# Last Q tile of chunk 0 placed around the shift products, chunk 3's side lists rebuilt, row tile 2's sums ahead of the norms, 17 fillers for 19

## The chip, the cores and the metric

The kernel runs on one core of a Trainium2 chip. The metric is the device time of one execution in microseconds. TensorE (PE) multiplies, its weight loads (PEld) run beside it; VectorE (DVE), ScalarE (ACT) and GpSimd (POOL) work on vectors; the queue of SyncE (SP) issues nearly all transfers, in order. The engines run beside each other, each takes its own instructions strictly in the order of the program, and they wait for each other by semaphores.

## The reference

One block of an adaptive-layernorm transformer, bf16: S = 2048 rows, D = 1024, F = 3584, 32 heads of 32.

```python
mod = (_silu(c) @ w_mod).reshape(c.shape[0], 6, 1, -1)
sa, ca, ga, sb, cb, gb = ...
h = _layernorm(x) * (1 + ca) + sa
q, k, v = h @ wqkv, split into heads
phi = lambda t: where(t > 0, t + 1, exp(t)) + 1e-06
o = (phi(q) @ (phi(k).T @ v)) / (phi(q) @ phi(k).sum(rows) + 1e-06)
x = x + ga * (o @ wo)
h = _layernorm(x) * (1 + cb) + sb
x = x + gb * ((silu(h @ w_gate) * (h @ w_up)) @ w_down)
```

The change touches the first layernorm and the Q and K projections with `phi`.

## The kernel before

**Tiles and stages.** The 2048 rows are 16 row tiles of 128 and 4 chunks of 512 columns of the transposed activations. `XRES` holds the rows; each row tile is normalized in place and transposed into `HT`, which has two buffers: chunk 0 and 2 in one, 1 and 3 in the other. `dt` counts the 8 slices of D. The scale and shift of the layernorm (`MODCOL`) are applied to the transposed tiles.

**The order.** The program is written out by hand, one instruction after another; a helper (`auto`, whose line L176 every row of the profile bears) records it, and `resolve` turns overlaps of SBUF ranges and uses of a PSUM bank into semaphore waits. A PSUM bank that another engine last used is waited for, whoever wrote or read. What stands first in the program stands first in the queue of its engine.

**Start (lines 628 to 661).** Fillers (`warm`, a 128x512 matmul of zeros) keep TensorE at work while the first four row tiles land. Tiles 0 and 2 get their sums on VectorE (`bn_stats` twice, an aggregate), tiles 1 and 3 on ScalarE (`act_stats`, two passes). `ln1_rstd1` and `ve_sums` send the variance to GpSimd for the power; `ln1_xn` and `ln1_xn_sum` are the norms; `tile_transposes` brings a tile to PSUM on TensorE. `mod_sc` computes columns of the modulation vector with one-column matmuls into bank 0, and `fin_ca`, `fin_sa` copy them out.

**Chunk 0, Q (`q_phase_chunk0`, line 773).** Seven Q tiles accumulate side by side in seven banks (`qb`) while scale and shift become known slice by slice; `q_part` is one Q tile times some slices. The slices 0 to 3 are multiplied unshifted; their shift enters as a bias from `bias_mm` (one-column matmuls into bank 0) and `bias_fin`. The eighth Q tile follows in bank 0. `h0_shift` shifts the slices for K. `q_phi` evacuates a Q tile on ScalarE (Exp, Relu), `q_min` and `q_add` finish it on VectorE. Row tiles 4 to 7 are normalized here and transposed by the DMA (`th_dma`).

**Chunk 0's K, then chunks 1 to 3.** A group is eight 512-column matmuls, 1.73 us. Chunk 0 has 8 K groups, each other chunk 8 K and 8 Q groups. `phi_evac` puts Exp (and Relu for Q) on ScalarE into one of four slots of `E1`; after every second group `phi_flush` finishes both on VectorE, for K with an instruction that reads PSUM and writes `PKT`. `next_bank` (line 703) says which PSUM bank a group gets.

**Side lists.** After group `gi`, the functions of the lists `kside`, `s1`, `s2`, `s3` under that number are written into the program (line 870): statistics and norms of later row tiles (`ln_half`, `ln1_xn`), their transposes, `th_mod` (scale and shift of a transposed slice, for chunk 3 on VectorE for even slices and ScalarE for odd ones), `macc` (a matrix-vector product for a further piece of the modulation vector, on VectorE), `macc_split` (its split into two bf16 parts and their transpose), loads of weights.

Of the kernel before, what the change touches and what calls it, by code (L numbers as in the profile page):

```python
# [5 lines left out]
FP32 = mybir.dt.float32  # L6
# [256 lines left out]
def bass_adaLN_cond__linear_attn_block__swiglu_ffn__prompt_kernel(  # L263
# [22 lines left out]
    with ExitStack() as es:  # L286
# [6 lines left out]
        def T(name, off, shape, dt):  # L293
            n = 1
            for s_ in shape[1:]:
                n *= s_
            assert off % 32 == 0 and off + n * mybir.dt.size(dt) <= ARENA, (name, off, shape)
            return nc.alloc_sbuf_tensor_at(name, shape, dt, offset=base + off)
# [47 lines left out]
        RL = T("rl", 188 * KB, [128, 4, 512], BF16)  # L346
        E1X = T("e1x", 192 * KB, [128, 4, 512], BF16)
        RLX = T("rlx", 196 * KB, [128, 4, 512], BF16)
        ACC = T("acc", 192 * KB, [128, D], FP32)
        MHL = T("mhl", 196 * KB, [128, 2, D], BF16)  # L350
        MHLT = T("mhlt", 192 * KB, [128, 2 * NDT, 128], BF16)
# [105 lines left out]
        def warm(n=1, bank=2):  # L457
            for _ in range(n):
                P.pe("matmul", out=PS[:, bank, :], lhsT=IDENT[:], rhs=E1[:, 0, :], start=True, stop=True)
# [23 lines left out]
        def ln1_xn(st, c0=0, c1=D):  # L483
            P.dve("tensor_scalar", out=XRES[:, st, c0:c1], in0=XRES[:, st, c0:c1],
                  scalar1=MV[:, st, 0:1], scalar2=RSTD[:, st:st + 1], op0=ALU.subtract, op1=ALU.mult)
# [22 lines left out]
        def mod_sc(w, c0, ms, kts=range(NDT)):  # L508
            for m in ms:
                for kt in kts:  # L510
                    P.pe("matmul", out=PS[:, 0, c0 + m:c0 + m + 1], lhsT=w[:, kt, m * 128:(m + 1) * 128],
                         rhs=SILUC[:, kt:kt + 1], start=mod_first[0], stop=(kt == NDT - 1), skip_group_check=True)
                    mod_first[0] = False
# [48 lines left out]
        def ln1_rstd1(st):  # L562
            P.dve("tensor_scalar", out=VE[:, st:st + 1], in0=MV[:, st, 1:2], scalar1=EPS, scalar2=None, op0=ALU.add)
            P.pool("tensor_tensor", out=RSTD[:, st:st + 1], in0=VE[:, st:st + 1], in1=NEGHALF[:, 0:1], op=ALU.pow)
# [58 lines left out]
        def ve_sums(st):  # L623
            P.dve("tensor_scalar", out=VE[:, st:st + 1], in0=SUMSQ[:, st:st + 1], scalar1=MV[:, st, 1:2], scalar2=EPS,
                  op0=ALU.add, op1=ALU.add)
            pool_pow(st)

        warm(13, bank=3)
        act_stats(1)
        act_stats(3)  # L630
        for f in s0_:
# [1 line left out]
        ln1_rstd1(0)  # L633
        msq_neg(1)
        s2_[0]()
        ln1_xn(0)
        tile_transposes(0)
        warm(5, bank=3)
        ve_sums(1)
        s2_[1]()  # L640
        s2_[2]()
        ln1_rstd1(2)
        ln1_xn_sum(1)
        tile_transposes(1)
        warm(1, bank=3)
        msq_neg(3)
        ln1_xn(2, 0, 512)
        ve_sums(3)
        ln1_xn(2, 512, D)
        tile_transposes(2)  # L650
        mod_sc(WCA, 8, range(2))
        ln1_xn_sum(3, 0, 512)
        ln1_xn_sum(3, 512, D)
        fin_ca(0, 2)
        tile_transposes(3)
        mod_sc(WCA, 8, range(2, 4))
        h0_first(0, "dve")
        h0_first(1, "dve")
        raw_copy(4, "dve")
# [43 lines left out]
        def next_bank():  # L703
            i = qk_ctr[0]
            qk_ctr[0] += 1
            return (1, 2, 3, 4, 6, 7, 5, 0)[i % 8] if i < 40 else i % 5 + 1

        def q_group(ch, nt):
            buf, bank = ch % 2, next_bank()
# [39 lines left out]
        def mod_row_b(bank, i, dst):  # L749
# [3 lines left out]
            P.wait_for("sp", [wr])  # L753
            P.dma("mdr%d" % i, dst[:], MDR[i].unsqueeze(0).to_broadcast([128, D]))

        def q_slot(nt):
            return (E1, RL) if nt < 4 else (E1X, RLX)

        def q_phi(nt, bank):
            for buf, fn_ in zip(q_slot(nt), (ACT.Exp, ACT.Relu)):  # L760
                P.act("activation", out=buf[:, nt % 4, :], in_=PS[:, bank, :], func=fn_, bias=BIASQ[:, nt:nt + 1])

        def q_min(nts):
            for nt in nts:
                e = q_slot(nt)[0][:, nt % 4, :]
                P.dve("tensor_scalar", out=e, in0=e, scalar1=1.0, scalar2=1e-6, op0=ALU.min, op1=ALU.add)

        def q_add(nts):
            for nt in nts:
                e, r = q_slot(nt)  # L770
                P.dve("tensor_tensor", out=PQT[:, nt, 0:512], in0=r[:, nt % 4, :], in1=e[:, nt % 4, :], op=ALU.add)

        def q_phase_chunk0():
            qb = [1, 2, 3, 4, 6, 7, 5]
            fin_ca(2, 2)
            for dt in (2, 3):
                h0_first(dt, "dve")
            for nts, dts in ((range(3), (0,)), (range(3), (1,)), ((3, 4, 5, 6), (0, 1))):
                for nt in nts:
                    q_part(nt, qb[nt], dts)  # L780
            for nt in range(7):
                if nt == 4:
                    mod_sc(WCA, 8, range(4, 8))
                    fin_ca(4, 4)
                    for dt in (4, 5):
                        h0_scale_only(dt)
                q_part(nt, qb[nt], (2, 3))
            act_stats(4, (0,))
            for nt in range(7):
                if nt == 6:  # L790
                    mod_sc(WSA, 0, range(6, 8))
                    fin_sa(6, 2)
                    for dt in (6, 7):
                        h0_scale(dt)
                q_part(nt, qb[nt], (4, 5))
            mod_sc(WSA, 0, range(4, 6))
            fin_sa(4, 2, True)
            for dt in (4, 5):
                h0_shift(dt)
            for nt in range(7):  # L800
                if nt == 2:
                    bias_mm((4, 5))
                q_part(nt, qb[nt], (6,))
            for nt in range(7):
                if nt == 1:
                    mod_sc(WSA, 0, range(4), range(4))
                if nt == 3:
                    mod_sc(WSA, 0, range(4), range(4, 8))
                    fin_sa(0, 4, True)
                    ln_ops[1][0]()  # L810
                if nt == 5:
                    bias_mm(range(4))
                    bias_fin()
                q_part(nt, qb[nt], (7,))
            ln_ops[1][1]()
            ln_ops[1][2]()
            ln1_rstd1(5)
            for i, dt in enumerate((4, 5, 0, 1, 2, 3, 6, 7)):
                P.pe("matmul", out=PS[:, 0, :], lhsT=WQK[:, dt, 896:1024], rhs=HT[:, 0, dt, :], start=(i == 0),
                     stop=(i == 7))  # L820
            for dt in range(4):
                h0_shift(dt)
            ln1_xn(5)
            th_dma(5)
            for nt in range(2):
                q_phi(nt, qb[nt])
            act_stats(4, (1,))
            for nt in range(2, 8):
                q_phi(nt, qb[nt] if nt < 7 else 0)
            for f in ln_ops[2]:  # L830
                f()
            act_var(4)
            pool_pow(4)
            for f in ln_ops[3]:
                f()
            ln1_rstd2(6)
            ln1_xn_sum(4)
            th_dma(4)
            q_min((0, 1))
            for st in (6, 7):  # L840
                ln1_xn(st)
                th_dma(st)
            q_add((0, 1))
            for nts in ((2, 3), (4, 5)):
                q_min(nts)
                q_add(nts)
            qk_ctr[0] = 0

        def add(d, k, f):
# [2 lines left out]
        kside = {}  # L852
        ln_ops = [ln1_stats_ops(4 + jj) for jj in range(4)]

        for c0 in (0, 256):
            for dt in range(NDT):
                add(kside, 1, lambda dt=dt, c0=c0: th_mod(1, dt, c0, c0 + 256))
        add(kside, 1, lambda: q_min((6, 7)))
        add(kside, 1, lambda: q_add((6, 7)))
        for jj, k in ((0, 3), (1, 4)):  # L860
            add(kside, k, lambda jj=jj: act_stats(10 + jj))
        q_phase_chunk0()
        for st in range(12, 16):
# [44 lines left out]
            add(s1, 2, lambda jj=jj: th_dma(8 + jj))  # L908
        for i, dt in zip([9, 9, 10, 10, 10, 11, 11, 11], range(NDT)):
            add(s1, i, lambda dt=dt: th_mod(2, dt))  # L910
        ln_half(3, s1, 8, 8, 11)
        for jj in range(4):
            add(s1, 13 + jj // 2, lambda jj=jj: ln1_xn(12 + jj))
            add(s2, 0, lambda jj=jj: th_dma(12 + jj))
        for dt in range(NDT):
            add(s2, 6 + dt, lambda dt=dt: th_mod(3, dt))
        for kt in range(NDT):
            add(s2, 4 + kt, lambda kt=kt: macc(STG, kt))
        add(s2, 13, macc_split)
        add(s2, 13, lambda: P.dma("stg1", STG[:], wmv[:, :, 4096:5120]))  # L920
        for kt in range(NDT):
            add(s3, 4 + kt, lambda kt=kt: macc(STG, kt))
        add(s3, 14, macc_split)
        add(s1, 7, lambda: P.pool("memset", ap=MROW[:], constant=0.0))
        add(s1, 7, lambda: P.pool("memset", ap=ZHL[:], constant=0.0))
        s3.setdefault(2, []).extend([mod_red, mod_row_a])
        add(s3, 12, lambda: mod_row_b(7, 0, GA_B))
        add(s3, 10, z_cols)
        chunk(1, s1)
# [326 lines left out]
```

## Time and profile before

| what | us |
|---|---|
| median of 3 runs | 827.82 (827.47 to 1765.51) |
| the profiled execution, its own time | 828.25 |
| its span, first to last instruction | 826.5 |
| TensorE busy | 821.8 |
| VectorE busy | 313.4 |
| ScalarE busy | 197.0 |
| GpSimd busy | 41.0 |

The span is cut into the start (to 12.2 us), chunk 0's Q (to 29.9), chunk 0's K (to 43.7), chunks 1, 2 and 3 (to 71.5, 99.1 and 126.8), the rest of the attention (to 195) and the gated feed-forward. A row of a timeline names its start, its length, the engine, the operation, what it writes and reads, and how many instructions are merged. Busy times are unions of spans; a matmul's span is longer than the spacing of two matmuls, since they are pipelined.

### The profile page before, as it was taken

Reading aid. Unit: us, or ns where it says so; the run is one execution under the profiler, and the core shown is the slowest. Engines: PE = TensorE matmul, PEld = TensorE weight load, DVE = VectorE, ACT = ScalarE, POOL = GpSimd, SP = SyncE. Lnnn points to the kernel's source line nnn. Section 1 sums busy time; section 2 is a strip of 40 time slices with the busy share of each in tenths; the row PEclk is TensorE's granted clock in tenths of the full one; section 3 lists DMA queues with packets and bytes.
Section 4 is the critical chain, followed back from the end, with each engine's and each line's share of the span. In section 5 each row is a group of like instructions: output and inputs, shape, how many; then the busy total and the mean of one; then the engine's idle time right before and its main releaser. Section 6 shows DMA issues by size and latency. Waiting matters only on the chain.

```text
span 826.5 us, 10519 instructions
## 1 busy us (share of the span) xinstructions
PE 821.8 (99%) x4322; PEld 376.3 (46%) x4322; DVE 313.4 (38%) x672; ACT 197.0 (24%) x338; POOL 41.0 (5%) x58
## 2 busy tenths in 40 slices
PE   8999999999999999999999999999999999999998
PEld 4544444444444444444444444444444444444444
DVE  5798988566945521121221112122111211221111
ACT  4658643223341111011111101111110111111011
POOL 1110000000130000020000003000000300000000
PEclk9999999999999999999999999999999999999999
DMA  9969666865697985600455580045557004553000
GB/s 314 289 144 222 167 165 147 178 177 205 155 255 241 296 249 152 169 26 26 134 152 151 151 177 25 20 133 152 151 153 182 27 19 125 152 152 87 0 26 26
DMA packets 199456, 119.32 MB, mean 144 GB/s; under 512 B 58088, under 2 KB 183152, under 8 KB 199408
## 3 DMA queue, kind: packets, MB, share of 16 engines
q1 hardware_dynamic: 199392, 118.65, 53.7%
q8 instruction: 34, 0.56, 0.3%
q14 instruction: 14, 0.11, 0.0%
q10 hardware_dynamic: 16, 0.00, 0.0%
HBM read 100.67 MB, written 4.33 MB: 127 GB/s over the span
## 4 chain that ended last, share of the span: by engine, by line
PE 98%; DMA 1%; ACT 0%; SPq 0%; DVE 0%; POOL 0%; issue 0%
PE ps L176 98%; DMA xres<-in_A_x_dram 1%; ACT ht L176 0%; SPq L176 0%; DVE xres L176 0%; POOL rstd L176 0%; DVE ve L176 0%
## 5 line engine op out<-in xcount | busy, mean ns | idle before, releaser
L176 PE MATMUL ps<-h2t,guu 128*128 128x512 bf16 x896 | 211.7, 379 | 0.0
L176 PE MATMUL ps<-h2t,gug 128*128 128x512 bf16 x896 | 211.7, 379 | 0.0
L176 DVE TENSOR_TENSOR at<-sg,ps 128x512 bf16<-128x512 bf16 x112 | 77.1, 688 | 282.7 <-PE ps L176 281.1
L176 ACT ACTIVATE sg<-ps 128x512 bf16<-128x512 f32 x112 | 66.9, 597 | 309.7 <-PE ps L176 309.7
L176 PEld LDWEIGHTS ps<-h2t,guu 128*128 128x128 bf16 x896 | 87.7, 98 | 105.7
L176 PEld LDWEIGHTS ps<-h2t,gug 128*128 128x128 bf16 x896 | 87.6, 98 | 105.5
L176 PE MATMUL ps<-wd_a,at 128*128 128x512 bf16 (+1 forms) x512 | 112.4, 377 | 0.0
L176 PE MATMUL ps<-ht,wqk 128*128 128x512 bf16 x512 | 112.1, 379 | 0.0
L176 PE MATMUL ps<-wd_b,at 128*128 128x512 bf16 (+1 forms) x384 | 85.0, 377 | 0.0
L176 DVE TENSOR_TENSOR ut<-att,gb_b 128x512 bf16<-128x512 bf16 (+1 forms) x32 | 14.6, 456 | 166.5 <-ACT att L176 166.5
L176 PEld LDWEIGHTS ps<-wd_a,at 128*128 128x128 bf16 x512 | 50.1, 98 | 59.7
L176 PEld LDWEIGHTS ps<-ht,wqk 128*128 128x128 bf16 x512 | 49.2, 98 | 58.9 <-DVE ht L176 1.0
L176 ACT ACTIVATE att<-ps 128x512 bf16<-128x512 f32 (+1 forms) x32 | 17.4, 591 | 182.1 <-PE ps L176 182.1
L176 PEld LDWEIGHTS ps<-wd_b,at 128*128 128x128 bf16 x384 | 37.6, 98 | 44.7
L176 PE MATMUL ps<-pk,xres 128*128 128x512 bf16 x256 | 56.2, 379 | 0.0
L176 PE MATMUL ps<-mw,pqt 128*128 128x512 bf16 x256 | 55.9, 379 | 0.0
L176 POOL TENSOR_SCALAR h2t<-h2t,modcol 128x512 bf16<-128x512 bf16 x32 | 26.4, 841 | 382.9 <-DMA h2t<-xn 382.9
L176 ACT ACTIVATE e<-ps 128x512 bf16<-128x512 f32 x56 | 33.3, 611 | 31.8 <-PE ps L176 16.3
L176 ACT ACTIVATE junk<-xres 128x1024 bf16<-128x1024 bf16 x26 | 27.6, 1063 | 46.5 <-DVE xres L176 34.2
L176 PEld LDWEIGHTS ps<-mw,pqt 128*128 128x128 bf16 x256 | 24.8, 98 | 30.0 <-issue 0.5
L176 PEld LDWEIGHTS ps<-pk,xres 128*128 128x128 bf16 x256 | 24.7, 98 | 29.9 <-issue 0.9
L176 DVE SCALAR_TENSOR_TENSOR xres<-ps,xres 128x512 bf16<-128x512 f32 x32 | 21.5, 688 | 11.5 <-PE ps L176 11.3
(111 smaller groups left out, 339.3 us busy)
## 6 DMA issues: line engine op xcount, KB each, us to landing
gug<-in_B_w_gate_dram SPq DMA_DIRECT2D x56, 512.0 KB, 3.9
guu<-in_B_w_up_dram SPq DMA_DIRECT2D x56, 512.0 KB, 5.2
xres<-in_A_x_dram SPq DMA_DIRECT2D x20, 256.0 KB, 4.3
stgx<-in_w_mod_dram SPq DMA_DIRECT2D x2, 2048.0 KB, 9.9
wd_a<-in_B_w_down_dram SPq DMA_DIRECT2D x4, 1024.0 KB, 7.2
out_dram<-xres SPq DMA_DIRECT2D x31, 128.0 KB, 1.7
rb<-recip_den SPq DMA_DIRECT2D x8, 384.0 KB, 8.7
xres<-in_A_x_dram SPq DMA_DIRECT2D x3, 1024.0 KB, 6.8
```

The costliest lines, as they stand in the source:

```text
L176: return getattr(e, method)(**kw)
```

## The change

- Start: 14 fillers ahead instead of 13, then 1 and 2 instead of 5 and 1. VectorE does the second half of tile 2's sums, tile 1's variance and tile 2's variance ahead of the norm of tile 0. Three instead of two columns of the scale are computed ahead of tile 3's transposes.
- Q tile 7 of chunk 0: it no longer has bank 0 but Q tile 0's, which ScalarE copies out to a new fp32 buffer `QRAW`; the shift products and the bias products are placed among its eight matmuls instead of among the seven last parts. Both ScalarE passes of row tile 4 come behind that copy, and its variance ahead of the bias. The Q tiles are evacuated in the order 1 to 7, 0.
- Behind them only two pairs of Q tiles are finished ahead of K; the other two come after K group 3. `th_mod(1)` has 12 instructions instead of 16. ScalarE's sums of tiles 10 and 11 come one K group later.
- `next_bank` has another order for the first 40 groups.
- The statistics of tiles 12 to 15 move from groups 8 to 11 of chunk 1 to groups 12 to 14, their norms to group 15 and chunk 2's group 0, their transposes behind group 1, `th_mod(3)` from chunk 2's groups 6 to 13 to groups 4 to 11. The split of the first `macc` moves from group 13 to 12, with the load that follows ahead of it; in chunk 3 `mod_red` moves from group 2 to 4, `macc` from 4 to 11 to 6 to 13.

```diff
@@ -346,6 +346,7 @@
         RLX = T("rlx", 196 * KB, [128, 4, 512], BF16)
+        QRAW = T("qraw", 202 * KB, [128, 512], FP32)
         ACC = T("acc", 192 * KB, [128, D], FP32)
@@ -625,7 +626,7 @@
 
-        warm(13, bank=3)
+        warm(14, bank=3)
         act_stats(1)
@@ -633,27 +634,27 @@
         s2_[0]()
+        s2_[1]()
+        ve_sums(1)
+        s2_[2]()
+        ln1_rstd1(2)
         ln1_xn(0)
         tile_transposes(0)
-        warm(5, bank=3)
-        ve_sums(1)
-        s2_[1]()
-        s2_[2]()
-        ln1_rstd1(2)
+        warm(1, bank=3)
         ln1_xn_sum(1)
         tile_transposes(1)
-        warm(1, bank=3)
+        warm(2, bank=3)
         msq_neg(3)
...
         tile_transposes(2)
-        mod_sc(WCA, 8, range(2))
+        mod_sc(WCA, 8, range(3))
         ln1_xn_sum(3, 0, 512)
         ln1_xn_sum(3, 512, D)
-        fin_ca(0, 2)
+        fin_ca(0, 3)
         tile_transposes(3)
-        mod_sc(WCA, 8, range(2, 4))
+        mod_sc(WCA, 8, range(3, 4))
         h0_first(0, "dve")
@@ -703,7 +704,11 @@
             qk_ctr[0] += 1
-            return (1, 2, 3, 4, 6, 7, 5, 0)[i % 8] if i < 40 else i % 5 + 1
+            if i < 24:
+                return (0, 2, 3, 4, 6, 7, 5, 1)[i % 8]
+            if i < 40:
+                return (0, 2, 3, 4, 6, 1, 7, 5, 0, 2, 3, 1, 4, 6, 7, 5)[i - 24]
+            return i % 5 + 1
 
@@ -753,26 +758,34 @@
 
+        QORD = (1, 2, 3, 4, 5, 6, 7, 0)
+
         def q_slot(nt):
-            return (E1, RL) if nt < 4 else (E1X, RLX)
-
-        def q_phi(nt, bank):
+            i = QORD.index(nt)
+            bufs = (E1, RL) if i < 4 else (E1X, RLX)
+            return [t[:, i % 4, :] for t in bufs]
+
+        def q_phi(nt, src):
             for buf, fn_ in zip(q_slot(nt), (ACT.Exp, ACT.Relu)):
-                P.act("activation", out=buf[:, nt % 4, :], in_=PS[:, bank, :], func=fn_, bias=BIASQ[:, nt:nt + 1])
+                P.act("activation", out=buf, in_=src, func=fn_, bias=BIASQ[:, nt:nt + 1])
 
...
             for nt in nts:
-                e = q_slot(nt)[0][:, nt % 4, :]
+                e = q_slot(nt)[0]
                 P.dve("tensor_scalar", out=e, in0=e, scalar1=1.0, scalar2=1e-6, op0=ALU.min, op1=ALU.add)
...
                 e, r = q_slot(nt)
-                P.dve("tensor_tensor", out=PQT[:, nt, 0:512], in0=r[:, nt % 4, :], in1=e[:, nt % 4, :], op=ALU.add)
+                P.dve("tensor_tensor", out=PQT[:, nt, 0:512], in0=r, in1=e, op=ALU.add)
+
+        def q_pair(i):
+            q_min(QORD[i:i + 2])
+            q_add(QORD[i:i + 2])
 
...
             qb = [1, 2, 3, 4, 6, 7, 5]
-            fin_ca(2, 2)
+            fin_ca(3, 1)
             for dt in (2, 3):
@@ -785,7 +798,6 @@
                 q_part(nt, qb[nt], (2, 3))
-            act_stats(4, (0,))
             for nt in range(7):
@@ -802,48 +814,46 @@
             for nt in range(7):
-                if nt == 1:
+                q_part(nt, qb[nt], (7,))
+                if nt == 0:
+                    P.act("activation", out=QRAW[:], in_=PS[:, qb[0], :], func=ACT.Copy)
+                    act_stats(4)
+            for i, dt in enumerate(range(NDT)):
+                if i == 1:
                     mod_sc(WSA, 0, range(4), range(4))
-                if nt == 3:
+                if i == 3:
                     mod_sc(WSA, 0, range(4), range(4, 8))
+                    ln_ops[1][0]()
                     fin_sa(0, 4, True)
-                    ln_ops[1][0]()
-                if nt == 5:
+                    ln_ops[1][1]()
+                    act_var(4)
+                    pool_pow(4)
+                if i == 5:
                     bias_mm(range(4))
                     bias_fin()
-                q_part(nt, qb[nt], (7,))
-            ln_ops[1][1]()
+                P.pe("matmul", out=PS[:, qb[0], :], lhsT=WQK[:, dt, 896:1024], rhs=HT[:, 0, dt, :], start=(i == 0),
+                     stop=(i == 7))
             ln_ops[1][2]()
             ln1_rstd1(5)
-            for i, dt in enumerate((4, 5, 0, 1, 2, 3, 6, 7)):
-                P.pe("matmul", out=PS[:, 0, :], lhsT=WQK[:, dt, 896:1024], rhs=HT[:, 0, dt, :], start=(i == 0),
-                     stop=(i == 7))
             for dt in range(4):
                 h0_shift(dt)
+            ln1_xn_sum(4)
+            th_dma(4)
             ln1_xn(5)
             th_dma(5)
-            for nt in range(2):
-                q_phi(nt, qb[nt])
-            act_stats(4, (1,))
-            for nt in range(2, 8):
-                q_phi(nt, qb[nt] if nt < 7 else 0)
+            for nt in QORD:
+                q_phi(nt, QRAW[:] if nt == 0 else PS[:, qb[nt % 7], :])
             for f in ln_ops[2]:
                 f()
-            act_var(4)
-            pool_pow(4)
             for f in ln_ops[3]:
...
             ln1_rstd2(6)
-            ln1_xn_sum(4)
-            th_dma(4)
-            q_min((0, 1))
+            q_min(QORD[0:2])
             for st in (6, 7):
...
                 th_dma(st)
-            q_add((0, 1))
-            for nts in ((2, 3), (4, 5)):
-                q_min(nts)
-                q_add(nts)
+            q_add(QORD[0:2])
+            q_pair(2)
             qk_ctr[0] = 0
@@ -852,12 +862,12 @@
 
-        for c0 in (0, 256):
-            for dt in range(NDT):
-                add(kside, 1, lambda dt=dt, c0=c0: th_mod(1, dt, c0, c0 + 256))
-        add(kside, 1, lambda: q_min((6, 7)))
-        add(kside, 1, lambda: q_add((6, 7)))
-        for jj, k in ((0, 3), (1, 4)):
+        for dt, c0, c1 in ([(dt, 0, 256) for dt in range(4)] + [(dt, 256, 512) for dt in range(4)]
+                           + [(dt, 0, 512) for dt in range(4, 8)]):
+            add(kside, 1, lambda dt=dt, c0=c0, c1=c1: th_mod(1, dt, c0, c1))
+        for i in (4, 6):
+            add(kside, 3, lambda i=i: q_pair(i))
+        for jj, k in ((0, 4), (1, 5)):
             add(kside, k, lambda jj=jj: act_stats(10 + jj))
@@ -908,22 +918,22 @@
             add(s1, i, lambda dt=dt: th_mod(2, dt))
-        ln_half(3, s1, 8, 8, 11)
+        ln_half(3, s1, 12, 12, 14)
         for jj in range(4):
-            add(s1, 13 + jj // 2, lambda jj=jj: ln1_xn(12 + jj))
-            add(s2, 0, lambda jj=jj: th_dma(12 + jj))
+            add(s1 if jj < 2 else s2, 15 if jj < 2 else 0, lambda jj=jj: ln1_xn(12 + jj))
+            add(s2, 1, lambda jj=jj: th_dma(12 + jj))
         for dt in range(NDT):
-            add(s2, 6 + dt, lambda dt=dt: th_mod(3, dt))
+            add(s2, 4 + dt, lambda dt=dt: th_mod(3, dt))
         for kt in range(NDT):
             add(s2, 4 + kt, lambda kt=kt: macc(STG, kt))
-        add(s2, 13, macc_split)
-        add(s2, 13, lambda: P.dma("stg1", STG[:], wmv[:, :, 4096:5120]))
+        add(s2, 12, lambda: P.dma("stg1", STG[:], wmv[:, :, 4096:5120]))
+        add(s2, 12, macc_split)
         for kt in range(NDT):
-            add(s3, 4 + kt, lambda kt=kt: macc(STG, kt))
+            add(s3, 6 + kt, lambda kt=kt: macc(STG, kt))
         add(s3, 14, macc_split)
...
         add(s1, 7, lambda: P.pool("memset", ap=ZHL[:], constant=0.0))
-        s3.setdefault(2, []).extend([mod_red, mod_row_a])
+        s3.setdefault(4, []).extend([mod_red, mod_row_a])
         add(s3, 12, lambda: mod_row_b(7, 0, GA_B))
```

## The prediction

> **What bounds the kernel now.** I read the page's first and fourth parts first, then the chain in order of time, the busy times by stage, the waits, and last the timelines of single engines from 12 to 130 us, where the diff works.
>
> ```profile
> PE 821.8 (99%) x4322; PEld 376.3 (46%) x4322; DVE 313.4 (38%) x672; ACT 197.0 (24%) x338; POOL 41.0 (5%) x58
> ...
> PE 98%; DMA 1%; ACT 0%; SPq 0%; DVE 0%; POOL 0%; issue 0%
> ```
>
> TensorE is busy for 821.8 of 826.5 us and is 98% of the chain that ends last. Outside it lie 4.7 us in all, so no rearrangement gains more than that unless it takes matmuls out, and this one takes out two fillers.
>
> ```profile
> 7.36 1.16 ACT ht L176 x2
> 8.52 0.02 issue
> 8.54 1.16 ACT ht L176 x2
> ...
> 10.70 0.43 DVE xres L176
> 11.12 0.05 issue
> 11.17 813.14 PE ps L176 x4262
> ```
>
> Up to 11.17 us the chain is row tile 3: its landing, ScalarE's two sums, VectorE's norm. From 11.17 on it is TensorE without a break.
>
> ```profile
> 29.88:43.69 13.81, 13.81 (x66) 6.27 (x64) 12.96 (x44) 13.78 (x26) 1.53 (x3) 1.00 1.16 238
> 43.69:71.50 27.81, 27.81 (x129) 12.36 (x128) 25.74 (x87) 18.16 (x34) 2.96 (x6) 1.00 0.81 147
> 71.50:99.10 27.60, 27.60 (x129) 12.51 (x128) 25.90 (x69) 19.87 (x36) 1.06 (x2) 1.00 0.84 217
> 99.10:126.80 27.70, 27.70 (x131) 12.60 (x129) 23.80 (x53) 13.46 (x24) 0.00 (x0) 1.00 0.52 134
> ```
>
> Stretches of chunks 0 to 3; columns are length, then busy PE, weight loads, DVE, ACT, POOL, then granted clock, DMA share, GB/s. VectorE has only 0.9, 2.1, 1.7 and 3.9 us idle per stretch. Nothing pushed back on it is made good before chunk 3, and it frees TensorE's banks.
>
> ```profile
> PEld ps L176 <- DVE ht L176: 1.0, 6, 0.2
> ...
> PEld ps L176 <- DVE pkt L176: 0.5, 1, 0.5
> ...
> PEld ps L176 <- DVE biasq L176: 0.4, 1, 0.4
> ```
>
> The weight loads' waits (total, times, longest) are what the change can remove. Most is hidden by the matmul in flight. By start-to-start spacing (0.216 us for a 512-column matmul), TensorE itself loses 0.04 us to `ht` at 45.00, 0.13 to `pkt` at 47.00, 0.04 to `biasq` at 27.89, and 0.08 at 25.66 to a `wsa` transfer: 0.29 in all.
>
> **The change, part by part.** The sum is made against the profiled execution: 828.25 us, a span of 826.5 and 1.75 around it. The median of the runs, 827.82, is 0.43 lower.
>
> *Start, to 12.2 us.* 19 fillers become 17. Fourteen end at 2.61 + 12 x 0.427 + 2 x 0.216 = 8.0 us. The moved sums (`bn_stats` 0.61 apart, aggregate and two small ones 0.4) put the norm of tile 0 at 7.2 to 7.75, 1.15 later than now, just under that cover; without it, it would cost up to 1.15. Tile 3's chain is untouched. Eight of the sixteen `mod_sc` matmuls (8 x 0.025 = 0.2) move into the 0.22 that TensorE waits before 11.17; the 24 then end at 11.31, `fin_ca` starts at 11.38 instead of 11.35, and the first Q matmul waits for it: +0.03.
>
> *Q tile 7.* All seven last parts run, then tile 7 in bank 1 with the 64 shift and bias products among its matmuls. Bank 1 is emptied by a ScalarE copy (0.6, as the rows of 591 to 600 ns), from 25.27 to 25.9; tile 7 needs it at 26.34, behind six matmuls of 0.216. Spare: 0.4. The products have 2 matmuls between them and the bias as now (0.06 wait stays), the `wsa` wait (0.08) and the `biasq` wait (0.04) go: K starts at 29.75 instead of 29.88, -0.12. VectorE now has, ahead of `bias_fin`, tile 5's first `bn_stats` (waiting for x5, 27.32 in the trace) and tile 4's variance, which waits for both ScalarE passes: x4 at 26.61 + 2.22 = 28.83, variance at 28.97, bias ready to be copied at 29.30. Spare 0.1, and what is queued behind are the four shifts and ScalarE's sixteen Q evacuations. Bounds: 0 to 0.5 (x5 waited 0.52); I take 0, the rows as they stand.
>
> *Chunk 0's K.* ScalarE starts the Q evacuations at 29.55 instead of 28.18 but has tile 4's second pass behind it: 16 x 0.57 ends at 38.67 against 38.35, +0.32. VectorE gets one Q pair more behind the first K flush (+1.07: two minima 0.20 apart, two adds 0.34 apart) and 8 + 4 instead of 16 `th_mod` (8 x 0.257 + 4 x 0.323 against 4.11, -0.76); it ends K at 51.7 against 51.07. The `th_mod` end at 44.7, needed by 45.05, and bank 3 is free at 45.7, needed at 47.0: both waits go, -0.17.
>
> *Chunk 1, ScalarE.* Row tiles 14 and 15 go from groups 8 and 9 to 12 and 13. Now they fill ScalarE from 62.43 to 68.46, while it would wait for the four transposes of chunk 2. After the change it does wait, from 63.9 to about 65.2 (last transpose issued 61.8, landing 3.4 later). Then 4 `th_mod` of 0.705, five Q evacuations of 0.955 and two statistics of 2.23 follow back to back and Q7's: 78.2 against 76.4.
>
> The queue's timeline, the landing row of tile `ht` for 75 to 90 us, and VectorE's timeline give the three points that the next sum moves:
>
> ```profile
> 75.63 5.36 SPq L176 DMA_TRANSPOSE ht<-xres  x4
> ```
> ```profile
> DMA to landing us min/median/max: 3.2/3.3/3.4
> ```
> ```profile
> 103.71 0.68 DVE L176 SCALAR_TENSOR_TENSOR pkt<-ps,e 128x512 bf16<-128x512 f32 x1
> ```
>
> *Chunk 3's input.* Norms 12 and 13 stand behind that last flush: 79.0 instead of 75.07. The transposes issue from 79.6, the fourth 4.05 later, landing 3.35 later: 87.0 against 83.0. But `th_mod(3)` moves forward, group 4 instead of 6. VectorE, in order, reaches it at 84.2 and stands until 87.05. Queued behind: all of `macc`, and every K and Q flush. From there to the evacuation of chunk 3's K0 it has no gap: 4 `th_mod` 1.29, 8 `macc` 0.66 + 7 x 1.2, two K flushes 2 x 1.63, four Q flushes 4 x 1.07, split 1.86, minima 0.40, the evacuation 0.68 = 20.8, so 107.9. In the trace it starts at 103.71 and ends at 104.4. K5 of chunk 3 takes the same bank (five are in turn there): due at 29.75 + 45 x 1.7265 = 107.4. Wait: 0.5. Before, 3.4 us were spare. Q3 of chunk 2, now in bank 1 behind K5, is due at 90.2, free at 89.8: no wait, 0.4 spare.
>
> Bounds of this cost: with a landing of 3.2 it is 0.3; with the 5.0 and 5.7 of the transposes at 35 and 37 us, which had weight loads beside them, Q3 waits too and it is 2.2 to 2.9; none at all if ScalarE is 0.5 quicker. I take 0.5: only a 256 KB load is near these.
>
> *Rest.* `macc` of chunk 3 two groups later ends VectorE about 1 us later; the sixth G group reuses its bank at 146.15, 3.9 after its evacuation (142.28). Nothing.
>
> Sum: +0.03 - 0.12 - 0.17 + 0.5 = +0.24. Profile 828.5, as a median 828.0.
>
> **A rule that speaks against it.** Row: matmul spacing is 0.427 us until 7.28 and 0.216 after; between 8.2 and 12.2 only six fillers (1.3 us) stand among transposes and tiny products, and it stays 0.216. The change leaves three there, and a gap of 0.58 before tile 2's second half where 0.15 is.
>
> The Trainium skill, "TensorE: Matmul & The Clock Gate", Part 1, says the array falls to half rate after an idle window of about 3.4 us in a free-running count, and Part 4 that transposes do not count as work. By that rule the start could fall back; the sum by it is the third rival's. This trace, warm through that stretch, does not bear it out.
>
> **Rivals.**
> - *First: no bank wait in chunk 3.* ScalarE or the transposes are 0.5 faster than added up. Net -0.26: 827.5. For it: the backlog is a long sum, and its spare changes sign within 0.5. Against: the same sum from the trace's own starts gives the old 103.71.
> - *Second, slower: the last transpose lands over 0.4 later than 87.0.* Then Q3 of chunk 2 waits as well, one for one. With 1 to 2 us: 828.0 + 1.0 to 2.0 = 829.0 to 830.0. For it: VectorE stands in order behind it. Against: all eight transposes of chunks 2 and 3 took 3.2 to 3.4.
> - *Third, slower: the clock falls back near 12 us.* Recovery as long as at the start (2.61 to 7.28) is 11 matmuls at 0.427: 11 x 0.211 = 2.3, so 830.3. For it: three fillers fewer there. Against: the trace stays at 0.216 with six.
> - *The change doesn't do what it says*: x4 or x5 lands later and Q tile 7's new order gives its 0.12 and 0.3 more back: 828.4, inside the forecast.
>
> **How the numbers follow.** Forecast 0.55 (with the last), first 0.26, second 0.14, third 0.03, anything else 0.02. Runs of one kernel spread by 0.8 (827.47 to 828.25), so each case has about 0.6 to both sides. The range goes from the first rival less 0.6, 826.9, to the second's 829.7. A difference of over 2% (16.6 us, about what a measurement of this kernel can tell from no change) needs three times all that TensorE ever waits to be gained, or a VectorE backlog of five times the largest bound above: 0.01 faster, 0.02 slower, 0.97 within.
>
> **What would show it.** Right: K0 of chunk 0 starts 0.1 earlier; no `pkt` wait at 47; ScalarE idle before 65; VectorE waiting for a transpose near 84 to 87; a `pkt` wait of TensorE near 107. Wrong: no gap on VectorE at 84, or TensorE waiting at 90; spacing of 0.427 after 8 us.

## The result, and the profile after

| what | before | after |
|---|---|---|
| median of 10 runs each, us | 827.85 (827.47 to 1765.51) | 829.87 (829.52 to 830.66) |
| after / before | | 1.0024, 95% interval 1.0016 to 1.0033 |
| profiled execution, its own time, us | 828.25 | 829.92 |
| its span, us | 826.5 | 828.0 |
| granted clock | 1.00 | 1.00 |

The change makes the kernel slower, by 2.0 us of 828. That is far inside 2%, and clear of no change by the interval. One run of before took 1765.51 us, for a reason that nothing here shows; the ratio leaves it out. The forecast was 828.0 with a range to 829.7: the time lies just above it.

The page of after, its busy times and the first line of its chain:

```profile
PE 816.1 (99%) x4241; PEld 375.9 (45%) x4320; DVE 312.0 (38%) x668; ACT 196.9 (24%) x339; POOL 40.9 (5%) x58
...
PE 94%; DVE 3%; DMA 2%; issue 1%; ACT 0%; DVEq 0%; ACTq 0%
```

TensorE shows 4241 matmuls for 4320 weight loads: 79 records are missing, spread evenly, and its busy time and its share of the chain are too low by them. The weight loads are complete, two fewer than before, as the fillers are. The first Q matmul is one of the missing: its weight load starts at 11.76 and the next one at 11.79, where before has 12.17 and 12.20 and the first Q matmul starts with the second load. So it started at 11.79; the record at 12.01 is the second matmul's. What is real in the second line is that VectorE and a transfer now stand in the chain, where TensorE alone stood from 11.17 us on.

Where the time went is read by stage. Chunks 1, 2 and 3 (columns as in the table of stretches above, length first):

```profile
43.36:70.98 27.62, 27.51 (x126) 12.47 (x128) 25.71 (x87) 16.32 (x31) 2.16 (x5) 1.00 0.74 142
70.98:98.60 27.62, 27.46 (x126) 12.51 (x128) 21.39 (x60) 19.69 (x38) 1.81 (x3) 1.00 0.79 206
98.60:128.40 29.80, 27.93 (x128) 12.43 (x129) 26.81 (x63) 15.11 (x28) 0.00 (x0) 1.00 0.52 141
```

Chunk 1 is 27.62 instead of 27.81, chunk 2 the same within 0.02, chunk 3 29.80 instead of 27.70: all of the loss is there. In chunk 2 VectorE is busy for 21.39 of 27.62 us instead of 25.90; that idle time did not hold TensorE up in chunk 2. The weight loads from 106 to 118 us show where it did (start, length; in brackets the idle time before and what ended it):

```profile
107.93 6.59 PEld L176 LDWEIGHTS ps<-ht,wqk 128*128 128x128 bf16 x32 [1.01 <-DVE pkt L176]
116.25 1.84 PEld L176 LDWEIGHTS ps<-ht,wqk 128*128 128x128 bf16 x10 [1.73 <-DVE pkt L176]
```

Two waits, both for a flush (`pkt`) that frees a bank. A weight load's idle time includes what is normal between two loads. By the starts of the matmuls, less the normal 0.216, TensorE itself loses **0.69 us at 107.0** (K5 of chunk 3, for the bank of K0) and **1.40 us at 114.6** (Q1, for the bank of K4). The ledger from the same spacing:

| piece | before | after | difference |
|---|---|---|---|
| first Q matmul starts | 12.20 | 11.79 | -0.41 |
| from there to K0 of chunk 0 | 17.68 | 17.76 | +0.08 |
| from K0 to the end of chunk 3's Q | 96.96 | 98.85 | +1.89 |
| first matmul behind chunk 3 | 126.84 | 128.40 | +1.56 |

The +1.89 are the two waits, 2.09, less the two of before (0.04 at 45.0, 0.13 at 47.0) that are gone. The -0.41 is a landing: row tile 3 lands at 6.93 instead of 7.33, and from there to the first Q matmul after takes 4.86 us and before 4.87. From the last row of the table to the end both kernels take 699.65 us, within 0.02.

VectorE of after, the rows that matter from 83 to 117 us:

```profile
84.04 0.08 DVE L176 DVE_READ_ACCUMULATOR pkt<-ps,e 128x1 f32 x1
86.91 0.41 DVE L176 TENSOR_SCALAR ht<-ht,modcol 128x512 bf16<-128x512 bf16 x1 [2.79 <-DMA ht<-xres]
...
107.18 0.68 DVE L176 SCALAR_TENSOR_TENSOR pkt<-ps,e 128x512 bf16<-128x512 f32 x1
...
110.03 0.08 DVE L176 DVE_READ_ACCUMULATOR pkt<-ps,e 128x1 f32 x1
112.70 2.29 DVE L176 TENSOR_REDUCE red<-mhlt 128x8 f32<-128x2048 bf16 x1 [2.59 <-DMA mhlt<-mhl]
...
115.50 0.68 DVE L176 SCALAR_TENSOR_TENSOR pkt<-ps,e 128x512 bf16<-128x512 f32 x1
```

In before the same two instructions have less than 0.1 us of idle time ahead of them:

```profile
85.41 0.41 DVE L176 TENSOR_SCALAR ht<-ht,modcol 128x512 bf16<-128x512 bf16 x1
...
105.09 2.29 DVE L176 TENSOR_REDUCE red<-mhlt 128x8 f32<-128x2048 bf16 x1
```

VectorE of after stands twice. At 84 us it stands 2.79 us at `th_mod(3)`, for chunk 3's transposes; K0's bank is then freed at 107.86 (107.18 + 0.68), and K5 starts right behind it, at 107.93. At 110 us it stands 2.59 us at `mod_red`, whose input `mhlt` is the transpose of the split; K4's flush stands behind that reduction in VectorE's queue and frees its bank at 116.18, and Q1 starts at 116.25. That second stand is what the prediction lacks. SP's queue shows why the transpose is late. Before:

```profile
100.69 1.91 SPq L176 DMA_TRANSPOSE mhlt<-mhl  x1
102.65 1.00 SPq L176 DMA_DIRECT2D stg<-in_w_mod_dram  x1
```

After:

```profile
102.81 0.38 SPq L176 DMA_DIRECT2D stg<-in_w_mod_dram  x1
104.74 5.86 SPq L176 DMA_TRANSPOSE mhlt<-mhl  x1
```

The 2048 KB load is now ahead. SP is held 5.86 us by the transpose instead of 1.91, and the transpose lands 7.9 us after its issue instead of 4.4. That is 112.6, and the reduction starts at 112.70.

### The profile page after: what moved, and what is told of

It is laid out like the page before. It is cut to its first block, busy times and chain, and to the rows that moved or that the text cites. A ratio compares the mean times of both kernels' runs of the same rounds, so it can differ in the third digit from the quotient of the medians.

```text
span 828.0 us, 10436 instructions
## 1 busy us (share of the span) xinstructions
PE 816.1 (99%) x4241; PEld 375.9 (45%) x4320; DVE 312.0 (38%) x668; ACT 196.9 (24%) x339; POOL 40.9 (5%) x58
## 4 chain that ended last, share of the span: by engine, by line
PE 94%; DVE 3%; DMA 2%; issue 1%; ACT 0%; DVEq 0%; ACTq 0%
PE ps L176 94%; DVE acc L176 1%; DMA mhlt<-mhl 1%; DVE pkt L176 1%; DMA ht<-xres 0%; DVE e L176 0%; DVE red L176 0%; DVE xres L176 0%; DMA cs<-in_c_dram 0%; DVE mhl L176 0%; DVE pqt L176 0%; DVE ht L176 0%; ACT e L176 0%; ACT rl L176 0%; ACT junk L176 0%
## 5 line engine op out<-in xcount | busy, mean ns | idle before, releaser
L176 PE MATMUL ps<-ht,wqk 128*128 128x512 bf16 x499 | 110.9, 379 | 2.9 <-DVE pkt L176 1.8
L176 PE MATMUL ps<-wd_a,at 128*128 128x512 bf16 (+1 forms) x502 | 111.9, 377 | 0.5
```

Of the source, the lines that this page charges most:

```text
L176: return getattr(e, method)(**kw)
```

## The experiments

Two theories, from the two stands. **A:** the transpose behind the load lands 3.5 us late, and `mod_red`, in order, holds K4's and K5's flushes behind it; this makes the 1.40. **B:** the late statistics, with `th_mod(3)` two groups earlier, make VectorE stand at 84 us; the backlog makes the 0.69, and it delays the split too, so that the 1.40 may hang on it as well. In the table, "waits" are TensorE's, by spacing, in chunks 2 and 3; the ratio is to the kernel before, run beside it.

| run | median us | before beside it | ratio, 95% | TensorE waits, us at |
|---|---|---|---|---|
| e1_load_behind_split | 828.24 | 828.12 | 1.0004 (0.9996 to 1.0013) | 0.70 at 106.9 |
| e2_scale_later | 827.88 | 828.12 | 1.0000 (0.9992 to 1.0009) | none |
| e3_before_load_ahead | 828.10 | 828.12 | 1.0 (0.9991 to 1.0009) | none |
| e4_both_undone | 827.80 | 828.12 | 0.9998 (0.9989 to 1.0007) | none |
| e5_front_alone | 828.45 | 827.79 | 1.0008 (0.9998 to 1.0018) | 0.48 at 72.0, 0.26 at 73.0 |
| e6_lists_alone | 829.43 | 827.79 | 1.0018 (1.0009 to 1.0027) | 1.03 at 114.9 |
| e7_stats_back | 828.72 | 827.79 | 1.0008 (0.9999 to 1.0018) | 0.52 at 72.0, 0.26 at 73.0 |
| e8_start_alone | 827.91 | 827.79 | 1.0002 (0.9993 to 1.0012) | none |
| e9_reduction_later | 828.44 | 828.02 | 1.0008 (0.9999 to 1.0017) | 0.71 at 106.9 |
| e10_scale_group5 | 828.28 | 828.02 | 1.0005 (0.9996 to 1.0013) | 0.51 at 113.9 |

Only e6 (and the change itself) can be told from the kernel before by its time. The others are told apart by the waits in their traces.

**The load put back behind the split** (changed kernel, one pair of lines exchanged):

```diff
-add(s2, 12, lambda: P.dma("stg1", STG[:], wmv[:, :, 4096:5120]))
 add(s2, 12, macc_split)
+add(s2, 12, lambda: P.dma("stg1", STG[:], wmv[:, :, 4096:5120]))
```

> The changed kernel with one pair of lines exchanged: the 2 MB load of the next modulation columns is issued behind the split's transpose again. Theory A (the transpose waits in the queue behind the load, 7.9 us to land instead of 4.4, and VectorE's reduction, in order, stands for it): the reduction no longer waits, TensorE's wait of 1.40 us at 114.6 us goes, the one of 0.69 at 107.0 stays; 828.4 us as a median. Theory B (VectorE's stand of 2.79 us for the transposes of chunk 3 pushes everything behind it, the order of the two transfers does not matter): both waits stay, 829.8 us.

Measured 828.24. SP's queue and VectorE of this run:

```profile
104.66 1.94 SPq L176 DMA_TRANSPOSE mhlt<-mhl  x1
106.64 0.98 SPq L176 DMA_DIRECT2D stg<-in_w_mod_dram  x1
```

```profile
109.94 2.28 DVE L176 TENSOR_REDUCE red<-mhlt 128x8 f32<-128x2048 bf16 x1
...
115.38 0.75 DVE L176 TENSOR_SCALAR acc<-stg,siluf 128x1024 f32<-128x1024 bf16 x1 [1.33 <-DMA stg<-in_w_mod_dram]
```

The transpose is issued at the same time as in the changed kernel and holds SP 1.94 us; the reduction starts without a wait, 2.76 us earlier. The 1.40 is gone, the 0.70 stays. The delay has moved to the transpose of `pkt` that is now behind the load: issued at 110.06, it lands 7.1 us later, and TensorE does not wait for it. VectorE now waits 1.33 for the load, behind the flushes, where no bank hangs on it. This is A, and the exchange of two lines is worth 1.4 us here.

**The scale and shift of chunk 3 put back to group 6** (changed kernel):

```diff
-    add(s2, 4 + dt, lambda dt=dt: th_mod(3, dt))
+    add(s2, 6 + dt, lambda dt=dt: th_mod(3, dt))
```

> The changed kernel with the scale and shift of chunk 3 back in groups 6 to 13 of chunk 2, everything else as changed. Theory B: VectorE does not stand at 84 us but does two macc there, all that follows comes 2.8 us earlier, and both waits of TensorE go: 827.8 us. Theory A alone: the transpose still takes 7.9 us behind the load, but it is issued 2.8 us earlier and lands at 109.7, just as VectorE gets to the reduction; so the 1.40 goes here as well, and only the 0.69 tells: it stays by A alone (828.5), goes by B (827.8).

Measured 827.88. VectorE has no stand near 84:

```profile
86.09 1.28 DVE L176 SCALAR_TENSOR_TENSOR acc<-stg,siluf,acc 128x1024 f32<-128x1024 bf16 x1
87.28 0.41 DVE L176 TENSOR_SCALAR ht<-ht,modcol 128x512 bf16<-128x512 bf16 x1
```

The same transposes are used at 87.28, with other work ahead. Both of TensorE's waits are gone, though the load is still ahead of the transpose, which still lands 7.6 us after its issue and still keeps VectorE standing 1.41 us. The split's transpose is issued 3.2 us earlier (101.50), the reduction starts at 109.14, and K4's bank comes free in time. So B makes the 0.69, and the 1.40 needs both: the late transpose, and the backlog that lets it come too late.

**The exchange alone, in the kernel before** (its lines under group 13):

```diff
+add(s2, 13, lambda: P.dma("stg1", STG[:], wmv[:, :, 4096:5120]))
 add(s2, 13, macc_split)
-add(s2, 13, lambda: P.dma("stg1", STG[:], wmv[:, :, 4096:5120]))
```

> The kernel before with the exchange alone: the 2 MB load issued ahead of the split's transpose. Theory A: the transpose lands at about 108.6 instead of 105.0, the reduction, which came just as it landed, stands 3.5 us, K3's and K2's evacuations with it, and K7 of chunk 3 waits about 1.0 us for its bank: 828.8 us. Theory B: nothing, 827.9.

Measured 828.10, no wait of TensorE. The time that A expected did not come. VectorE's row:

```profile
107.39 2.29 DVE L176 TENSOR_REDUCE red<-mhlt 128x8 f32<-128x2048 bf16 x1 [2.37 <-DMA mhlt<-mhl]
```

The stand is there, 2.37 us, but the transpose landed 6.7 us after its issue and not 7.9. K2's flush, the one behind the reduction here, ends at 110.88, and the group that takes its bank is due at 99.10 + 7 x 1.727 = 111.19. The load was issued 3.2 us ahead of the transpose here, and 1.9 us ahead in the changed kernel, so more of it was done. At 7.9 the group would have been 0.9 late. So the stand comes here too, and 0.3 us of spare hid it.

**Both undone** (the edits of e1 and e2 together).

> The changed kernel with both undone: load behind the transpose, scale and shift of chunk 3 in groups 6 to 13. By A and B together no wait of TensorE between 60 and 128 us is left (at most 0.1 at the last slices of chunk 3's first group), so what the front of the change gains shows: 827.5 to 827.8 us, 0.1 to 0.4 below the kernel before. If another cause holds, some of the 2.0 us stays.

Measured 827.80: the fastest of the set, 2.1 us under the changed kernel, and not distinguishable from the kernel before (0.9989 to 1.0007). What is left of the change, the start, Q tile 7 and the lists of chunk 0, reaches the end of chunk 3's Q at 126.30 instead of 126.84 in the trace, 0.44 of it by an earlier first Q matmul (11.76). That is too little to be seen in the time.

**The front alone**: the changed kernel with the statistics, norms, transposes, `th_mod(3)`, split, load, `macc` and `mod_red` at the numbers of before.

```diff
-ln_half(3, s1, 12, 12, 14)
+ln_half(3, s1, 8, 8, 11)
...
-    add(s2, 4 + dt, lambda dt=dt: th_mod(3, dt))
+    add(s2, 6 + dt, lambda dt=dt: th_mod(3, dt))
...
-s3.setdefault(4, []).extend([mod_red, mod_row_a])
+s3.setdefault(2, []).extend([mod_red, mod_row_a])
```

> The changed kernel with the lists of chunks 1 to 3 as before (statistics of tiles 12 to 15 in groups 8 to 11, their transposes in chunk 2's group 0, scale and shift from group 6, split in 13 ahead of the load); start, Q tile 7, chunk 0's lists and the banks as changed. Theory (A and B: all of the loss lies in those lists): no evacuation wait of TensorE after 100 us. Added up from the rows, ScalarE's statistics then stand ahead of chunk 2's scale and shift and TensorE, which is 0.3 us earlier, may meet slices 5 and 7 of chunk 2's first group 0.2 to 0.7 us early near 72 us: 827.6 to 828.1 us. Rival (the front costs too, for example by the copy of Q tile 0): over 828.6.

Measured 828.45, a little above what was expected and under the rival's 828.6; TensorE does not wait in chunk 3. Weight loads of this run near 72 us:

```profile
72.72 0.23 PEld L176 LDWEIGHTS ps<-ht,wqk 128*128 128x128 bf16 x2 [0.81 <-ACT ht L176]
73.42 2.49 PEld L176 LDWEIGHTS ps<-ht,wqk 128*128 128x128 bf16 x13 [0.47 <-ACT ht L176]
```

TensorE starts chunk 2 and waits 0.48 and 0.26 us for slices 5 and 7, which ScalarE shifts. With the front as changed and the statistics early, ScalarE is late with chunk 2's `ht`. The late statistics of the change take that wait away.

**The lists alone**: the same lines the other way, the kernel before with the lists of the change.

> The kernel before with the changed lists of chunks 1 to 3 alone, banks as before. Theory: VectorE stands for chunk 3's transposes near 84 us, the split's transpose takes about 7.9 us behind the load, and TensorE waits 1.1 to 1.4 us near 114.6 and 0 to 0.7 near 107: 829.0 to 829.9 us. Rival (the loss needs the new banks or the new front too): 828.1 us.

Measured 829.43, within what was expected; of the parts, 1.03 at 114.9 is a little under its 1.1 to 1.4, and there is nothing at 107. The transpose lands in 7.9 us, the reduction stands 2.6 us. The loss sits in the lists: with the old front they lose 1.6 us against the kernel beside them, the whole change 2.0. The trace shows 1.03 of the 1.6 as waits; the rest lies inside the interval.

**Statistics, norms and transposes back, the rest as changed**:

```diff
-ln_half(3, s1, 12, 12, 14)
+ln_half(3, s1, 8, 8, 11)
...
-    add(s1 if jj < 2 else s2, 15 if jj < 2 else 0, lambda jj=jj: ln1_xn(12 + jj))
-    add(s2, 1, lambda jj=jj: th_dma(12 + jj))
+    add(s1, 13 + jj // 2, lambda jj=jj: ln1_xn(12 + jj))
+    add(s2, 0, lambda jj=jj: th_dma(12 + jj))
```

> The changed kernel with the statistics, norms and transposes of tiles 12 to 15 back in their old groups, but scale and shift of chunk 3 still from group 4 and the load still ahead of the split. Theory: the transposes land near 83, VectorE does not stand, the wait at 107 goes; the split comes 3 us earlier, its transpose still takes 7 to 8 us but lands by 109.3, so the wait at 114.6 goes too; 827.6 to 828.1 us. If B's stand has another cause than the late statistics, 829.9 stays.

Measured 828.72, above the expected 828.1. Both waits in chunk 3 are gone as expected, with `th_mod(3)` still in group 4 and the load still ahead (the transpose lands in 7.9 us, VectorE stands 0.5). In their place come e5's waits at 72 and 73, and 0.41 at 20.95 for a `wsa` transfer. VectorE still stands at `th_mod(3)`, but only 1.62 us, to 83.61 instead of 2.79 to 86.91: the stand comes from the late statistics and the early use together, and with the statistics put back it ends 3.3 us earlier and costs no bank.

**The start alone, in the kernel before**: the three blocks of fillers, the sums and variance of tile 2 ahead of the norms, and the three columns of the scale.

```diff
-warm(13, bank=3)
+warm(14, bank=3)
...
-warm(5, bank=3)
-ve_sums(1)
+ve_sums(1)
...
-mod_sc(WCA, 8, range(2))
+mod_sc(WCA, 8, range(3))
...
-fin_ca(0, 2)
+fin_ca(0, 3)
```

> The kernel before with the changed start alone (14, 1 and 2 fillers, the sums of tile 2 ahead of the norms, three columns of the scale). Theory: row tile 3's landing and ScalarE's sums set the first Q matmul in both, so within 0.1 us of the kernel before from landing to Q: 828.0 to 828.2 us. Clock rival: spacing of 0.427 us somewhere after 8 us and 2 us more.

Measured 827.91. A matmul spacing of 0.427 does not come back after 8 us, here or in the changed kernel. The first Q matmul starts at 12.09 (its record is missing too, and the loads show it). Row tile 3 landed at 6.69, so that is 5.40 us after the landing, not within 0.1 of the 4.87 of before as expected; what else held it was not taken apart. TensorE then waits 0.31 at 21.3 and 0.10 at 25.9 for `wsa` transfers, so the earlier start does not reach K. The start's own part can't be read from single traces.

**The reduction two groups later** (changed kernel, ahead of the other work of group 6):

```diff
-s3.setdefault(4, []).extend([mod_red, mod_row_a])
+s3.setdefault(6, [])[0:0] = [mod_red, mod_row_a]
```

> The changed kernel with the reduction two groups later in chunk 3 (group 6, ahead of that group's macc), the load still ahead of the split's transpose. Theory A in its narrow form (it is not the late transpose itself that costs, but that VectorE stands for it with the evacuations of K4 and K5 queued behind): the transpose still takes 7.9 us, VectorE evacuates K4 and K5 before it stands, TensorE's wait of 1.40 us at 114.6 goes, the 0.69 at 107 stays: 828.4 us. If the transfers themselves slow TensorE or the banks otherwise, 829.8 stays.

Measured 828.44, as A expected. VectorE of this run:

```profile
110.62 0.68 DVE L176 SCALAR_TENSOR_TENSOR pkt<-ps,e 128x512 bf16<-128x512 f32 x1
...
111.23 0.69 DVE L176 SCALAR_TENSOR_TENSOR pkt<-ps,e 128x512 bf16<-128x512 f32 x1
...
112.90 2.29 DVE L176 TENSOR_REDUCE red<-mhlt 128x8 f32<-128x2048 bf16 x1 [0.98 <-DMA mhlt<-mhl]
```

The transpose is as late as ever (8.3 us), but K4's and K5's flushes now stand ahead of the reduction and free their banks at 111.3 and 111.9. The wait at 114 is gone, the 0.71 at 107 is untouched. It is therefore not the transfer as such, nor DMA traffic beside the matmuls, but what is queued behind the waiting instruction.

**The scale and shift of chunk 3 from group 5** (half way between the change and e2):

```diff
-    add(s2, 4 + dt, lambda dt=dt: th_mod(3, dt))
+    add(s2, 5 + dt, lambda dt=dt: th_mod(3, dt))
```

> The changed kernel with scale and shift of chunk 3 one group later (from group 5 instead of 4), everything else as changed, the load ahead too. By the sum: VectorE passes one macc and the evacuations of K4 and K5 before it stands for the transposes, so 2.3 us of the 2.8 are used; the split comes 2.1 us earlier, the transpose lands at 110.4 as VectorE gets there, and both waits of TensorE go: 827.7 us, as in the kernel with it in group 6. If the loss goes in proportion to the groups, half of it, about 828.8, stays.

Measured 828.28, above the expected 827.7. VectorE waits 0.52 us at 86.72 instead of 2.79, and the wait at 107 is gone. But 0.51 is left at 113.9: the split is 1.9 us earlier than in the changed kernel, its transpose lands 8.2 us later (111.1), and VectorE stands 2.84 us there. The backlog was mostly gone and the exchange of load and transpose still cost half a microsecond.

## Why the prediction was wrong, point by point

- **The step that failed** is "*Rest.* ... Nothing." The part lists `macc` and the sixth G group; the exchange of the 2048 KB load and the split's transpose in SP's queue, which the diff shows, has no price anywhere in the sum, and `mod_red` is not checked against its input. By the landing of before (4.4) the transpose would have come at 104.74 + 4.4 = 109.1, ahead of VectorE's arrival at 110.1: no stand. It came at 112.6. The step was worth 1.40 (e1: gone with the exchange undone; e9: gone with the flushes ahead of the reduction). With this term the sum would have been 828.5 + 1.4 = 829.9 for the profiled execution (829.92 measured), and 829.4 as a median (829.87). That the first agrees to hundredths is luck: by the ledger the start came 0.44 below its term, Q tile 7 0.20 and chunk 3's input 0.19 above theirs. The trace of before could have priced it. The load there takes 8.6 us from issue to landing, the transpose ahead of it 4.4; and a transpose behind loads is there too, issued at 30.71, which lands 7.6 us later and 1.0 us after the last of those loads. By these rows, as an estimate, a load issued at 102.81 puts the transpose behind it at 102.81 + 8.6 + 1.0 = 112.4.
- **A rule that bears on the failed step.** The Trainium skill, "DMA: Bandwidth & Descriptors", section "Queues, rings and completion order", says that a DMA engine takes the descriptors of one ring in the order in which they stand there, and that the DMAs SP issues share one such row of rings. The traces agree: behind the load the transpose took 6.7 to 8.3 us to land over seven kernels, 4.4 ahead of it in before, e1, e4, e5 and e8.
- **Chunk 3's input: right, and the size near.** VectorE was forecast to stand from 84.2 to 87.05 and stood from 84.12 to 86.91. K5 was to wait 0.5 at 107.4 and waited 0.69 at 107.0; K0's bank was to be free at 107.9 and was free at 107.86. e2 shows that this stand is the cause.
- **ScalarE in chunk 1: right.** Idle from 63.9 to about 65.2 was forecast; the row is below. It evacuates Q7 at 77.45 to 78.54, forecast 78.2.

```profile
65.35 0.81 ACT L176 ACTIVATE ht<-ht,modcol 128x512 bf16<-128x512 bf16 x1 [1.18 <-DMA ht<-xres]
```

- **Chunk 0's K: right.** The waits at 45.0 and 47.0 (0.17 together) are gone. In e1, e4 and e9, with the same front, 0.07 to 0.18 is left near 44.3, so this is a matter of a tenth.
- **Q tile 7: not confirmed.** Forecast -0.12 from the first Q matmul to K0, by two waits of before (`wsa` at 25.66, `biasq` at 27.89). Both are gone, but after has a new one, 0.20 at 21.0 for the first of the three `wsa` transfers, which lands at 21.4; +0.08 in all. Without a `wsa` wait the interval is 17.54 to 17.55 in e2, e4, e5, e9 and e10. It is 17.54 too in e3 and e6, which keep the old order. So the 0.12 were waits that come and go from one trace to the next, and what the new order itself gains is not shown.
- **Start: right from the landing on.** Forecast +0.03; from row tile 3's landing to the first Q matmul it measured -0.01. The tile landed 0.40 earlier, and it lands anywhere from 6.43 to 7.33 in the twelve traces (6.69 and 7.03 in e3 and e6, which keep the old start), so this 0.40 can't be put down to the change. Nor is the 4.87 a constant: over the twelve the interval is 4.86 to 5.72.
- **First rival, no bank wait: did not happen.** e4 shows the time it would give, 827.80 (forecast 827.5).
- **Second rival: its time came, by another way.** It gave 829.0 to 830.0 through late transposes and a wait of Q3 of chunk 2. Those transposes landed as forecast, and TensorE waits nowhere between 47 and 107 us, so the time agrees by chance.
- **Third rival, the clock: did not happen.** The spacing stays 0.216 with three fillers between 8 and 12 us. (The granted clock reads 1.00 there, but it reads 1.00 from 2.5 to 6.7 us as well, where the fillers are 0.427 apart; so the spacing decides.) By the rule of the Trainium skill, "TensorE: Matmul & The Clock Gate", Parts 1 and 4, a window filled with transposes could have let it fall; in after and in e8 it did not. The longest stretch of after without a 512-column matmul is 2.3 us (9.5 to 11.8), against 2.3 in before (9.9 to 12.2), so the change tests no longer one.
- **Last, x4 or x5 late: not seen.** K0 of chunk 0 starts at 29.55.
- **Slips in the working.** 2.61 + 12 x 0.427 + 2 x 0.216 is 8.17, not 8.0; nothing hangs on it. The range ends at 829.7, while the second rival's own time runs to 830.0, and no reason is given; 829.87 lies between the two. The working takes 2% as about what can be told from no change; the interval above is 0.7 us to each side.

The spread of the late transpose, 6.7 us in e3 and 7.6 to 8.3 in the six others, follows the load. In all seven kernels it lands 1.7 to 1.9 us after the load does; the load takes 7.95 to 8.31 us, and the transpose is issued 1.9 us behind it in five, 2.1 in e2 (7.6) and 3.2 in e3 (6.7).

What stays open: e5's and e7's late `ht` at 72 us was seen, not taken apart further, and what the new start and the new order of Q tile 7 are worth by themselves is not resolved.

## What to carry to other kernels

When a diff exchanges two lines that both go to one DMA queue, price each transfer behind the other's bytes, and then ask which engine waits for the delayed one in order and what stands behind that wait. A backlog on an in-order engine costs nothing until it meets its next due time: here undoing the stand at 84 us alone (e2) took both waits away, and the exchange alone cost nothing in the kernel before (e3). So check each later wait against the shifted times, not against those of the old trace. Put the frees of banks ahead of an instruction that waits for a transfer, not behind it.

## What the runs showed that was not expected

A 512 KB transpose (128x2048 bf16) behind a 2048 KB load costs the issuing queue too: SP was held 4.7 to 6.2 us by its issue, instead of 1.9 us. In all seven kernels SP came free 0.2 to 0.3 us before the load landed. The DMA issues of after from 100 to 116 us (tile, engine, operation and count, KB where known, us from issue to landing):

```profile
stg<-in_w_mod_dram SPq DMA_DIRECT2D x1, 2048.0 KB, 8.1
mhlt<-mhl SPq DMA_TRANSPOSE x1, 7.9
```

The load lands at 102.81 + 8.1 = 110.9, the transpose at 112.6. Ahead of the load, in before, the transpose took 4.4 us, and the load 8.6: putting the load first brought the load in only 0.5 us sooner after its issue, and the transpose 3.5 us later.
